# A gated decode step: work items of one head against work items of two heads, and all weights through the cache's buffers

## The chip, the cores and the metric

The kernel runs on one core of a Trainium2 chip. The metric is the device time of one execution in microseconds (us). The profile's span, from the first to the last instruction, lies a little under it.

## The reference

For two sequences (B = 2), one new token each (D = 640), the block mixes two branches with a gate. Branch `a` is attention over a cache of 4,096 positions with 32 heads of 128; branch `b` is a SiLU feed-forward layer. All data is 32-bit floats.

```python
g = sigmoid((x * gate_w).sum(-1, keepdims=True))
# a: x [2,1,640], k_cache and v_cache [2,32,4096,128], wq [640,4096], wo [4096,640]
q = (x @ wq).reshape(B, 1, H, Dh).transpose(0, 2, 1, 3)
scores = einsum("bhqd,bhkd->bhqk", q, k_cache) * Dh ** -0.5
o = einsum("bhqk,bhkd->bhqd", softmax(scores), v_cache)
a = o.transpose(0, 2, 1, 3).reshape(B, 1, H * Dh) @ wo
# b: w1 [640,1728], w2 [1728,640]
b = silu(x @ w1) @ w2
out = g * a + (1 - g) * b
```

The two caches are 268.4 MB of the 298 MB that are read.

## The kernel before, in words

A work item is one head of one sequence, so there are 64 items, ordered by head and then by sequence. An item's K is 4,096 x 128 numbers, laid out as 128 partitions with 32 consecutive positions each, so every partition takes one contiguous run of 16 KB; V is laid out the same way. `load_k` (L199) and `load_v` (L207) issue these loads from SyncE's queue (SP).

For each item the kernel does this:

- `scores_mul`: the query times K, elementwise. GpSimd takes the last 8 of the 32 position columns (L220), VectorE the first 24 (L223), reading the query from PSUM.
- `scores_sum`: VectorE sums over the 128 numbers of each position (L227) and takes the maximum in each partition (L229).
- `peak` and `weights`: TensorE brings the 128 maxima into one row (L233, tile `mt`), VectorE reduces it (L235, `mx`), TensorE spreads the result to all partitions (L240, `mb`), ScalarE copies it (L242, `nb`) and computes the exponentials with their sums (L244, into the `pz` tile).
- `total` and `invert`: TensorE sums over the partitions (L256, `tot`), VectorE inverts (L261).
- `values`: 8 products of the weights with V, four position columns at a time, each to one of four groups of 32 PSUM partitions (L272, `pv`).
- `combine` and `scale`: ScalarE copies `pv` to SBUF (L283, `osb`); four small products pick the four diagonal blocks and give the head's output as a column (L286, `po`); VectorE scales it (L293).
- `project`: the output columns of both sequences times the head's 128 rows of `wo`, added to one accumulator `acc` in PSUM (L108) over all heads and over the feed-forward layer.

In the records every 32-bit matrix product is two records.

The queries of two heads are made by `queries` (L185) from `wq`, in four calls of three or two products spread over the four previous items; the columns of x are spread to 128 copies (`xb`), so that the query appears in every partition. `ffn_in` (L137) multiplies x with `w1`, in pieces of two column blocks between the items 14 and 39; `ffn_act` applies SiLU; `ffn_out` accumulates the hidden values times `w2` at the end.

There are three pools of buffers: five for K (also used for `w2` at the end), four for V, four for weights of 10 KB per partition. `wq` comes in eight loads with runs of 2 KB, `wo` in eight with runs of 2.5 KB, `w1` in four with runs of 2 KB and 768 bytes, `w2` in eight with runs of 2.5 KB. The order on every engine is written out by hand in the loop at the end of the kernel: in round i, K of item i is loaded and scored, the softmax of item i - 1 is done, and V of item i - 3 is loaded and used (`LAG = 3`). In the last round the loads of `w2` and of the last `wo` are issued, and the accumulations over them end the kernel.

Of the kernel before, what the change touches and what calls it, by code (L numbers as in the profile page):

```python
# [15 lines left out]
def tile_gated_decode(  # L16
# [12 lines left out]
    nc = tc.nc  # L29
# [16 lines left out]
    work = ctx.enter_context(tc.tile_pool(name="work", bufs=3))  # L46
# [3 lines left out]
    ps_s = ctx.enter_context(tc.tile_pool(name="ps_s", bufs=3, space=bass.MemoryType.PSUM))  # L50

# [4 lines left out]

    wq_v = wq.rearrange("(p j) n -> p j n", j=J)
    w1_v = w1.rearrange("(p j) f -> p j f", j=J)
    WQ = 4 * DH
    wq_sb = {}  # L60

    def load_wq(s):
        t = wpool.tile([P, J, WQ], F32, tag="w", name="wq_sb")
        nc.sync.dma_start(t, wq_v[:, :, s * WQ : (s + 1) * WQ])
        wq_sb[s] = t
# [5 lines left out]
    nscale = const.tile([1, P], F32, name="nscale")  # L71
    nc.vector.memset(nscale, -SCALE)
    sel = const.tile([P, 4], F32, name="sel")
    nc.vector.reduce_sum(sel, ident.rearrange("p (a b) -> p b a", b=32)[:, :4, :], axis=AX.X)
    NPZ = 4
    pz = []
# [5 lines left out]
    xb = const.tile([P, B, J, P], F32, name="xb")  # L82
    nc.vector.tensor_copy(xb, xs[:, :, :, None].to_broadcast([P, B, J, P]))
    g = const.tile([P, B], F32, name="g")
    gc = const.tile([P, B], F32, name="gc")

    def gates():
        gb = wpool.tile([P, J, P], F32, tag="w", name="gb")
# [4 lines left out]
        ge = work.tile([P, B], F32, name="ge", bufs=1)  # L93
# [8 lines left out]
    NMM = H + NF  # L102
# [14 lines left out]
    o_first = const.tile([P, 32], F32, name="o_first")  # L117
    nc.vector.memset(o_first, 0.0)

    hT = const.tile([P, NF, B], F32, name="hT")  # L120

    W1, PH = {}, {}

    def load_w1(n0, n1):
        f0, f1 = FC[n0][0], FC[n1 - 1][0] + FC[n1 - 1][1]
        t = wpool.tile([P, J, WQ], F32, tag="w", name="w1_sb")
        nc.sync.dma_start(t[:, :, : f1 - f0], w1_v[:, :, f0:f1])
        for n in range(n0, n1):
            W1[n] = t[:, :, FC[n][0] - f0 : FC[n][0] - f0 + FC[n][1]]

    def ffn_in(n0, n1):
        m = FC[n0][1]
        ph = ps_s.tile([P, 512], F32, tag="sm", name="ph")
        for n in range(n0, n1):
            c = (n - n0) * B
            for j in range(J):
                nc.tensor.matmul(  # L137
                    ph[:m, c : c + B], W1[n][:, j, :], xs[:, :, j], start=(j == 0), stop=(j == J - 1)
                )
        PH[n0] = ph  # L140

    def ffn_act(n0, n1):
        m, k = FC[n0][1], n1 - n0
        ph = PH[n0][:m, : k * B].rearrange("p (n b) -> p n b", b=B)
        e = work.tile([P, 4, B], F32, name="he", bufs=2)
        e = e[:m, :k, :]
        nc.scalar.activation(e, ph, AF.Exp, scale=-1.0)
        nc.vector.tensor_scalar_add(e, e, 1.0)
        nc.vector.reciprocal(e, e)
        nc.vector.tensor_mul(e, e, gc[:m, None, :].to_broadcast([m, k, B]))  # L150
        nc.vector.tensor_mul(hT[:m, n0:n1, :], ph, e)  # L151

    TAIL = ((NF - 1, NF), (0, 4), (4, 7), (7, 9), (9, 10), (10, 11), (11, 12), (12, 13))

    def ffn_load(n0, n1):
        if FC[n0][1] == P:
            t = kpool.tile([P, n1 - n0, D], F32, tag="k", name="w2_sb")
            nc.sync.dma_start(t, w2[n0 * P : n1 * P, :].rearrange("(n p) d -> p n d", p=P))
        else:
            f, m = FC[n0]  # L160
            t = kpool.tile([P, 1, D], F32, tag="k", name="w2_sb")
            nc.sync.dma_start(t[:m, 0, :], w2[f : f + m, :])
        return n0, n1, t

    def ffn_out(n0, n1, t):
        for n in range(n0, n1):
            m = FC[n][1]
            accumulate(hT[:m, n, :], t[:m, n - n0, :])

    items = [(h, b) for h in range(H) for b in range(B)]  # L170
    N = len(items)
    CV = C - C // 4
    LATE = H - 4
    qsb = {}
    qps, K, V, S, M, R, O, WO = {}, {}, {}, {}, {}, {}, {}, {}

    QUNITS = [(b, j0, j1) for b in range(B) for j0, j1 in ((0, 3), (3, J))]

    def queries(hp, u):
        s, lo = divmod(hp * 2 * DH, WQ)  # L180
        if u == 0:
            qps[hp] = ps_q.tile([P, B, 2 * DH], F32, name="q")
        b, j0, j1 = QUNITS[u]
        for j in range(j0, j1):
            nc.tensor.matmul(  # L185
                qps[hp][:, b, :],
                xb[:, b, j, :],
                wq_sb[s][:, j, lo : lo + 2 * DH],
                start=(j == 0),
                stop=(j == J - 1),  # L190
            )
        if u == len(QUNITS) - 1:
            qsb[hp] = work.tile([P, B, 2 * DH], F32, name="qsb", bufs=2)
            nc.scalar.copy(qsb[hp], qps[hp])  # L194

    def load_k(i):
        h, b = items[i]
        K[i] = kpool.tile([P, C, DH], F32, tag="k", name="k")
        nc.sync.dma_start(K[i], kc[b, h].rearrange("(p c) d -> p c d", c=C))  # L199

    def load_v(i):
        h, b = items[i]
        V[i] = vpool.tile([P, C, DH], F32, name="v")
        src = vc[b, h].rearrange("(p c) d -> p c d", c=C)
        step = C // 4 if i == N - 1 else C
        for c in range(0, C, step):
            nc.sync.dma_start(V[i][:, c : c + step, :], src[:, c : c + step, :])  # L207
        if h % 4 == 0 and b == 0 and h < LATE:
            load_wo(h // 4)

    def load_wo(n):
        t = wpool.tile([P, 4, D], F32, tag="w", name="wo_sb")
        nc.sync.dma_start(t, wo[4 * n * DH : 4 * (n + 1) * DH, :].rearrange("(n p) d -> p n d", p=P))
        WO[n] = t

    def scores_mul(i):
        h, b = items[i]
        lo = (h % 2) * DH
        q = qps[h // 2][:, b, lo : lo + DH]
        nc.gpsimd.tensor_mul(  # L220
            K[i][:, CV:, :], K[i][:, CV:, :], qsb[h // 2][:, b, lo : lo + DH][:, None, :].to_broadcast([P, C - CV, DH])
        )
        nc.vector.tensor_mul(K[i][:, :CV, :], K[i][:, :CV, :], q[:, None, :].to_broadcast([P, CV, DH]))  # L223

    def scores_sum(i):
        S[i] = work.tile([P, C], F32, name="s")
        nc.vector.reduce_sum(S[i], K[i], axis=AX.X)  # L227
# [3 lines left out]
    def peak(i):  # L231
        mt = ps_s.tile([P, 512], F32, tag="sm", name="mt")
        nc.tensor.matmul(mt[:1, :P], M[i], ident, start=True, stop=True)  # L233
        mx = work.tile([1, 1], F32, name="mx")
        nc.vector.reduce_max(mx, mt[:1, :P], axis=AX.X)  # L235
        M[i] = mx

    def weights(i):
        mb = ps_s.tile([P, 512], F32, tag="sm", name="mb")
        nc.tensor.matmul(mb[:, :1], nscale, M[i], start=True, stop=True)  # L240
        nb = work.tile([P, 1], F32, name="nb")
        nc.scalar.copy(nb, mb[:, :1])  # L242
        rs = work.tile([P, 1], F32, name="rs")
        nc.scalar.activation(  # L244
            pz[i % NPZ][:, :, :4],
            S[i].rearrange("p (g c) -> p g c", c=4),
            AF.Exp,
            bias=nb,
            scale=SCALE,
            accum_out=rs,  # L250
        )
        R[i] = rs

    def total(i):
        t = ps_s.tile([P, 512], F32, tag="sm", name="tot")
        nc.tensor.matmul(t[:, :1], ones, R[i], start=True, stop=True)  # L256
        R[i] = t

    def invert(i):
        r = work.tile([P, 1], F32, name="rinv", bufs=5)  # L260
        nc.vector.reciprocal(r, R[i][:, :1])  # L261
        R[i] = r

    PV = {}

    def values(i, g0, g1):
        if g0 == 0:
            PV[i] = ps_pv.tile([P, 4 * DH], F32, name="pv")
        v = V[i].rearrange("p (g c) d -> p g (c d)", c=4)
        for gr in range(g0, g1):  # L270
# [7 lines left out]
            )  # L278

    def combine(i):  # L280
        h, b = items[i]
# [117 lines left out]
```

## Time and profile before

| | us |
|---|---|
| median of 3 runs | 719.47 (719.46 to 719.49) |
| profiled execution: span | 716.6 |
| what the median has beside the span | 2.9 |
| busy: TensorE matmul / VectorE / GpSimd / ScalarE | 526.8 / 543.1 / 152.3 / 85.5 |
| mean granted TensorE clock | 0.686 |
| DMA | 298.72 MB in 33,280 packets |

The time of the profiled execution itself is given by its span; the time of the runs counts a little more at the two ends. Busy times are sums over instructions. A "group" row of the profile gives line, engine, operation, output and inputs, count, then busy us and mean ns of one, then the idle time of the engine just before these instructions and what ended most of it. A row of the timeline gives start, duration, engine, line, operation, operands and how many instructions are merged in it. The rows of stretches give for each stretch the busy time of each engine, the granted clock, the share of the 16 DMA engines' time and the rate in GB/s.

### The profile page before, as it was taken

Reading aid. Unit: us, or ns where it says so; the run is one execution under the profiler, and the core shown is the slowest. Engines: PE = TensorE matmul, PEld = TensorE weight load, DVE = VectorE, ACT = ScalarE, POOL = GpSimd, SP = SyncE. Lnnn points to the kernel's source line nnn. Section 1 sums busy time; section 2 is a strip of 40 time slices with the busy share of each in tenths; the row PEclk is TensorE's granted clock in tenths of the full one; section 3 lists DMA queues with packets and bytes.
Section 4 is the critical chain, followed back from the end, with each engine's and each line's share of the span. In section 5 each row is a group of like instructions: output and inputs, shape, how many; then the busy total and the mean of one; then the engine's idle time right before and its main releaser. Section 6 shows DMA issues by size and latency. Waiting matters only on the chain.

```text
span 716.6 us, 6927 instructions
## 1 busy us (share of the span) xinstructions
PE 526.8 (74%) x2758; PEld 283.9 (40%) x2758; DVE 543.1 (76%) x426; ACT 85.5 (12%) x282; POOL 152.3 (21%) x74
## 2 busy tenths in 40 slices
PE   2358778778767797689978776876787486785686
PEld 2234444336434273343644434432343143342233
DVE  0798989895798857978569995978787778889930
ACT  0001111101111101110011111111011011101110
POOL 0503131121312113111131221212221221222200
PEclk9655767666588765855557766688657667557668
DMA  9999999999999999999999999999999999999996
GB/s 354 412 431 426 430 418 420 421 425 433 415 423 421 427 429 414 424 420 429 431 416 423 416 431 427 420 423 429 424 428 419 423 427 431 423 429 430 424 378 251
DMA packets 33280, 298.72 MB, mean 417 GB/s; under 512 B 2968, under 2 KB 3616, under 8 KB 16992
## 3 DMA queue, kind: packets, MB, share of 16 engines
q1 hardware_dynamic: 32824, 298.27, 99.6%
q8 instruction: 22, 0.36, 0.2%
q10 hardware_dynamic: 424, 0.01, 0.0%
q14 instruction: 10, 0.08, 0.0%
HBM read 298.26 MB, written 0.01 MB: 416 GB/s over the span
## 4 chain that ended last, share of the span: by engine, by line
DMA 43%; DVE 29%; PE 24%; ACT 2%; issue 1%; SPq 1%; ACTq 0%; DVEq 0%
DMA v<-in_A_v_cache_dram 39%; DVE s L227 14%; DVE k L223 12%; PE pv L272 7%; PE q L185 6%; PE ph L137 4%; PE po L286 3%; DMA w_sb<-in_B_w_dram 3%; PE acc L108 2%; DMA wq_sb<-in_A_wq_dram 2%; PE mb L240 1%; ACT osb L283 1%; SPq L199 1%; PE mt L233 1%; ACT qsb L194 1%
## 5 line engine op out<-in xcount | busy, mean ns | idle before, releaser
L227 DVE TENSOR_REDUCE s<-k 128x32 f32<-128x4096 f32 x64 | 281.4, 4397 | 0.1
L223 DVE TENSOR_TENSOR k<-k,q 128x3072 f32<-128x3072 f32 x64 | 214.4, 3349 | 77.1 <-ACT qsb L194 53.8
L220 POOL TENSOR_TENSOR k<-k,qsb 128x1024 f32<-128x1024 f32 x64 | 150.6, 2358 | 526.8 <-DMA k<-in_A_k_cache_dram 273.2
L272 PE MATMUL pv<-v,pz 128*32 128x512 f32 x1024 | 211.9, 870 | 56.5 <-DMA v<-in_A_v_cache_dram 56.4
L185 PE MATMUL q<-wq_sb,xb 128*128 128x256 f32 x320 | 128.0, 555 | 12.6 <-DMA wq_sb<-in_A_wq_dram 12.6
L286 PE MATMUL po<-sel,osb 128*128 128x1 f32 x512 | 86.0, 289 | 21.0 <-ACT osb L283 21.0
L185 PEld LDWEIGHTS q<-wq_sb,xb 128*128 128x128 f32 x320 | 82.2, 276 | 25.6 <-issue 12.6
L286 PEld LDWEIGHTS po<-sel,osb 128*128 128x128 f32 x512 | 80.5, 240 | 27.5 <-ACT osb L283 27.2
L240 PEld LDWEIGHTS mb<-mx,nscale 1*128 1x128 f32 x128 | 27.3, 264 | 122.9 <-issue 64.7
L242 ACT COPY nb<-mb 128x1 f32<-128x1 f32 x64 | 10.2, 159 | 467.1 <-PE mb L240 467.1
L272 PEld LDWEIGHTS pv<-v,pz 128*32 128x32 f32 x1024 | 34.9, 131 | 68.6 <-issue 59.0
L235 DVE TENSOR_REDUCE mx<-mt 1x1 f32<-1x128 f32 x64 | 17.5, 274 | 52.6 <-PE mt L233 52.6
L240 PE MATMUL mb<-mx,nscale 1*128 1x1 f32 x128 | 32.7, 322 | 33.4 <-DVE mx L235 33.2
L256 PEld LDWEIGHTS tot<-rs,ones 128*128 128x128 f32 x128 | 23.6, 231 | 77.9 <-issue 41.4
L233 PE MATMUL mt<-ident,m 128*1 128x128 f32 x128 | 33.2, 354 | 18.1 <-DVE rinv L261 16.8
L283 ACT COPY osb<-pv 128x512 f32<-128x512 f32 x64 | 37.5, 586 | 59.2 <-PE pv L272 59.2
L108 PE MATMUL acc<-wo_sb,oT 128*2 128x160 f32 x248 | 19.5, 406 | 28.1 <-DVE oT L293 27.9
L256 PE MATMUL tot<-rs,ones 128*128 128x1 f32 x128 | 29.1, 296 | 1.4 <-ACT pz L244 1.4
L137 PE MATMUL ph<-xs,w_sb 128*128 128x2 f32 (+1 forms) x140 | 26.6, 321 | 4.6 <-DVE hT L151 4.6
L137 PEld LDWEIGHTS ph<-xs,w_sb 128*128 128x128 f32 (+1 forms) x140 | 26.2, 289 | 4.8 <-issue 4.8
L233 PEld LDWEIGHTS mt<-ident,m 128*1 128x1 f32 x128 | 9.7, 97 | 40.1 <-DVE rinv L261 19.7
L293 DVE TENSOR_SCALAR oT<-po,rinv,g 128x1 f32<-128x1 f32 x62 | 16.1, 260 | 12.4 <-PE po L286 12.4
(37 smaller groups left out, 99.6 us busy)
## 6 DMA issues: line engine op xcount, KB each, us to landing
k<-in_A_k_cache_dram SPq DMA_DIRECT2D x64, 2048.0 KB, 36.1
v<-in_A_v_cache_dram SPq DMA_DIRECT2D x63, 2048.0 KB, 34.5
wq_sb<-in_A_wq_dram SPq DMA_DIRECT2D x8, 1280.0 KB, 37.6
wo_sb<-in_A_wo_dram SPq DMA_DIRECT2D x8, 1280.0 KB, 29.2
w_sb<-in_B_w_dram SPq DMA_DIRECT2D x4, 1280.0 KB, 11.8
v<-in_A_v_cache_dram SPq DMA_DIRECT2D x4, 512.0 KB, 18.2
w_sb<-in_B_w_dram SPq DMA_DIRECT2D x4, 320.0 KB, 9.5
w_sb<-in_B_w_dram SPq DMA_DIRECT2D x1, 960.0 KB, 15.9
```

The costliest lines, as they stand in the source:

```text
L108: nc.tensor.matmul(acc[32 * n : 32 * n + m, :], lhsT, w[:, n * W : (n + 1) * W], start=(done[0] == 0), stop=(done[0] == NMM - 1),)
L137: nc.tensor.matmul(ph[:m, c : c + B], W1[n][:, j, :], xs[:, :, j], start=(j == 0), stop=(j == J - 1))
L185: nc.tensor.matmul(qps[hp][:, b, :], xb[:, b, j, :], wq_sb[s][:, j, lo : lo + 2 * DH], start=(j == 0), stop=(j == J - 1),)
L220: nc.gpsimd.tensor_mul(K[i][:, CV:, :], K[i][:, CV:, :], qsb[h // 2][:, b, lo : lo + DH][:, None, :].to_broadcast([P, C - CV, DH]))
L223: nc.vector.tensor_mul(K[i][:, :CV, :], K[i][:, :CV, :], q[:, None, :].to_broadcast([P, CV, DH]))
L227: nc.vector.reduce_sum(S[i], K[i], axis=AX.X)
L233: nc.tensor.matmul(mt[:1, :P], M[i], ident, start=True, stop=True)
L240: nc.tensor.matmul(mb[:, :1], nscale, M[i], start=True, stop=True)
L256: nc.tensor.matmul(t[:, :1], ones, R[i], start=True, stop=True)
L272: nc.tensor.matmul(PV[i][32 * q : 32 * q + 32, :], pz[i % NPZ][:, gr, :], v[:, gr, :], start=(gr < 4), stop=(gr >= NG - 4),)
L283: nc.scalar.copy(osb.rearrange("p c d -> p (c d)"), PV[i])
L286: nc.tensor.matmul(po[:, :1], osb[:, c, :], sel[:, c : c + 1], start=(c == 0), stop=(c == 3))
```

## The change

A work item is now two neighbouring heads of one sequence: 32 items. The 2 x 4,096 positions lie in 128 partitions with 64 consecutive positions each, head one in partitions 0 to 63 and head two in 64 to 127, and each partition takes one contiguous run of 32 KB.

All large loads go through one pool of five slabs of 34,560 bytes per partition, in a fixed order (`stream`); `pump` issues the next load as soon as the program has passed the last use of the load five places earlier (`spend`). The order is: wq for six pairs of heads, w1, then K and V of each item in turn, with wq's second chunk after item 7, three groups of wo after item 13, wq's third chunk after item 18, and after the last item three groups of wo, w2 and two groups of wo. V of an item follows its K at once. The last 64 rows of w2 come in a load of their own at the end. Weights are laid out so that a partition's run is contiguous: wq 4 or 6 KB, wo 10 KB, w1 34,560 bytes (all of a partition's five rows), w2 33,280 bytes (13 rows).

The computation follows. VectorE multiplies columns 0 to 23, then (after the step on the maximum of the item before) 24 to 43; GpSimd takes 20 columns. The maximum is taken for each half of the partitions; `mb` is made by two products, and the exponentials by two activations of 64 partitions. `values` has 16 products per item, with the two heads' weights in different columns. `po` has two columns.

The queries are made as rows (`query_rows`, 32 columns of weights, up to 512 columns of wq at a time), for a whole chunk of wq at once, and one small product per sequence and pair of heads spreads them over the partitions (`query`). `ffn_in` does all of w1 at once before the first item, reading the weight columns `n:FM:FR` at a step of 13, since w2 is now laid out with 13 rows per partition. For wo with four rows per partition, `project` works on a group of four heads and reorders the heads' outputs with 16 small products against columns `n:P:4` of the identity (`pp`), a copy by ScalarE (`oP`), and then accumulates. `project(0..2)` is called in round 14, all others after the loop. The core of the diff:

```diff
-    kpool = ctx.enter_context(tc.tile_pool(name="kpool", bufs=5))
-    vpool = ctx.enter_context(tc.tile_pool(name="vpool", bufs=4))
-    wpool = ctx.enter_context(tc.tile_pool(name="wpool", bufs=4))
+    slabs = ctx.enter_context(tc.tile_pool(name="slabs", bufs=SLOTS))
...
+    stream = [("wq", 0), ("w1", 0)]
+    for i in range(N):
+        stream += [("k", i), ("v", i)]
+        if i == 7:
+            stream.append(("wq", 1))
+        if i == 13:
+            stream.append(("wo", 0))
+        if i == 18:
+            stream.append(("wq", 2))
+    stream += [("wo", 1), ("w2", 0), ("wo", 2)]
...
+    def pump():
+        while nxt[0] < len(stream):
+            m = nxt[0]
+            if m >= SLOTS and stream[m - SLOTS] not in spent:
+                return
+            t = slabs.tile([P, SLAB], F32, tag="slab", name=stream[m][0])
+            sub(*stream[m], t)
...
+    def ffn_in():
+        w = T["w1", 0].rearrange("p (j f) -> p j f", j=J)
...
+                cols = w[:, j, n:FM:FR] if n < FR else w[:, j, FM:F]
...
+        spend("w1", 0)
...
+    def query_rows(n, part):
...
+                    nc.tensor.matmul(
+                        ps[32 * hh : 32 * hh + 32, : (e - s) * DH],
+                        xz[:, j, :],
+                        w[:, j, s:e, hh, :],
...
+    def project(grp):
+        pp = ps_s.tile([P, 512], F32, tag="sm", name="pp")
+        for n in range(4):
+            for h in range(4):
+                nc.tensor.matmul(
+                    pp[32 * h : 32 * h + 32, n * B : (n + 1) * B],
+                    ident[:, n : P : 4],
+                    O[grp][:, h, :],
...
+        nc.scalar.copy(oP[:, :, :B], pp[:, : 4 * B].rearrange("p (n b) -> p n b", b=B))
...
+    gates()
+    query_rows(0, 0)
+    query_rows(0, 1)
+    query(0)
+    ffn_in()
+    late = {
+        8: [lambda: query_rows(1, 0), lambda: query_rows(1, 1)],
+        14: [lambda: project(0), lambda: project(1), lambda: project(2)],
+        19: [lambda: query_rows(2, 0), lambda: query_rows(2, 1)],
+    }
+    for i in range(N + 1):
+        if i < N:
+            mul(i, 0)
+        if i >= 1:
             peak(i - 1)
+            weights(i - 1)
+        if i < N:
+            mul(i, 1)
+            scores(i)
+            if i + 1 < N and items[i + 1][1] == 0:
+                query(items[i + 1][0])
+        if i >= 1:
             total(i - 1)
+            values(i - 1)
+            combine(i - 1)
+            invert(i - 1)
+            scale(i - 1)
         for f in late.get(i, []):
             f()
+    for grp in range(3, 6):
+        project(grp)
+    nc.sync.dma_start(w2t, w2[FM:, :])
+    ffn_out()
+    project(6)
+    project(7)
+    accumulate(hT[:FT, FR, :], w2t)
```

More of the change, by code (lines that the diff above doesn't have):

```diff
@@ L50, in tile_gated_decode, with sub, spend @@
     ps_s = ctx.enter_context(tc.tile_pool(name="ps_s", bufs=3, space=bass.MemoryType.PSUM))
+    order = ctx.enter_context(tc.manual_schedule())
+    items = [(hp, b) for hp in range(HP) for b in range(B)]
+    N = len(items)
+    QCH = ((0, 6), (6, 12), (12, HP))
+    WOG = ((0, 3), (3, 6), (6, 8))
+    stream = [("wq", 0), ("w1", 0)]
[8 more added lines that the diff above has]
+    stream += [("wo", 1), ("w2", 0), ("wo", 2)]
+    T = {}
+    spent = set()
+    nxt = [0]
+    def sub(what, n, t):
+        if what in ("k", "v"):
+            hp, b = items[n]
+            src = (kc if what == "k" else vc)[b, 2 * hp : 2 * hp + 2]
+            nc.sync.dma_start(
+                t[:, : C * DH], src.rearrange("h s d -> (h s d)").rearrange("(p c) -> p c", p=P)
+            )
+        elif what == "wq":
+            p0, p1 = QCH[n]
+            w = (p1 - p0) * 2 * DH
+            nc.sync.dma_start(
+                t[:, : J * w].rearrange("p (j n) -> p j n", j=J),
+                wq.rearrange("(p j) n -> p j n", j=J)[:, :, p0 * 2 * DH : p1 * 2 * DH],
+            )
+        elif what == "w1":
+            nc.sync.dma_start(t[:, : J * F], w1.rearrange("(p j) f -> p (j f)", j=J))
+        elif what == "w2":
+            nc.sync.dma_start(t[:, : FR * D], w2[:FM, :].rearrange("(p n) d -> p (n d)", n=FR))
+        else:
+            g0, g1 = WOG[n]
+            for g in range(g0, g1):
+                nc.sync.dma_start(
+                    t[:, (g - g0) * 4 * D : (g - g0 + 1) * 4 * D],
+                    wo[g * 4 * DH : (g + 1) * 4 * DH, :].rearrange("(p n) d -> p (n d)", n=4),
+                )
+    def pump():
[5 more added lines that the diff above has]
+            sub(*stream[m], t)
+            T[stream[m]] = t
+            nxt[0] += 1
+    def spend(what, n):
+        spent.add((what, n))
+        pump()
     xs = const.tile([P, B, J], F32, name="xs")
@@ L70, in tile_gated_decode @@
     nc.vector.memset(ones, 1.0)
[L71 to L76, printed above, removed]
+    nsc = const.tile([1, 2, P], F32, name="nsc")
+    nc.vector.memset(nsc, 0.0)
+    for hh in range(2):
+        nc.vector.memset(nsc[:, hh, hh * HALF : (hh + 1) * HALF], -SCALE)
+    sel = const.tile([P, 8], F32, name="sel")
+    nc.vector.reduce_sum(sel, ident.rearrange("p (a b) -> p b a", b=32)[:, :8, :], axis=AX.X)
+    spread = const.tile([HALF, B, P], F32, name="spread")
+    for b in range(B):
+        for hh in range(2):
+            nc.vector.tensor_copy(
+                spread[:, b, hh * HALF : (hh + 1) * HALF],
+                ident[:HALF, 32 * hh + b : 32 * hh + b + 1].to_broadcast([HALF, HALF]),
+            )
+    NPZ = 2
+    pz, rs2 = [], []
     for i in range(NPZ):
@@ L115, in accumulate @@
         done[0] += 1
[L117 to L129, printed above, removed]
@@ L153, in tile_gated_decode @@
[L153 to L163, printed above, removed]
@@ L196, in load_k @@
[L196 to L209, printed above, removed]
@@ new lines, in ffn_in, with ffn_out @@
+        spend("w1", 0)
+    def ffn_out():
+        w = T["w2", 0]
+        for n in range(FR):
+            accumulate(hT[:, n, :], w[:, n * D : (n + 1) * D])
+        spend("w2", 0)
+    qrow, qps, qsb = {}, {}, {}
+    def query_rows(n, part):
+        p0, p1 = QCH[n]
+        np_ = p1 - p0
+        w = T["wq", n][:, : J * np_ * 2 * DH].rearrange("p (j q h d) -> p j q h d", j=J, h=2, d=DH)
+        if part == 0:
+            qrow[n] = work.tile([HALF, 6 * DH], F32, name="qrow")
+        s, e = ((0, 4), (4, np_))[part]
+        if e > s:
+            ps = ps_s.tile([P, 512], F32, tag="sm", name="qr")
+            for j in range(J):
+                for hh in range(2):
+                    nc.tensor.matmul(
+                        ps[32 * hh : 32 * hh + 32, : (e - s) * DH],
+                        xz[:, j, :],
+                        w[:, j, s:e, hh, :],
+                        start=(j == 0),
+                        stop=(j == J - 1),
+                    )
+            nc.scalar.copy(qrow[n][:, s * DH : e * DH], ps[:HALF, : (e - s) * DH])
+        if part == 1:
+            spend("wq", n)
@@ new lines, in query @@
+    def query(hp):
+        n = next(k for k, (a, z) in enumerate(QCH) if a <= hp < z)
+        c = (hp - QCH[n][0]) * DH
+        qps[hp] = ps_q.tile([P, B, DH], F32, name="q")
+        for b in range(B):
+            nc.tensor.matmul(
+                qps[hp][:, b, :], spread[:, b, :], qrow[n][:, c : c + DH], start=True, stop=True
+            )
+        qsb[hp] = work.tile([P, B, DH], F32, name="qsb")
+        nc.scalar.copy(qsb[hp], qps[hp])
+    CA, CV = 24, 44
+    S, M, R, PV, PO, O = {}, {}, {}, {}, {}, {}
@@ new lines, in kview, with mul @@
+    def kview(i):
+        return T["k", i][:, : C * DH].rearrange("p (c d) -> p c d", d=DH)
+    def mul(i, part):
+        hp, b = items[i]
+        k = kview(i)
+        if part == 0:
+            nc.gpsimd.tensor_mul(
+                k[:, CV:, :], k[:, CV:, :], qsb[hp][:, b, None, :].to_broadcast([P, C - CV, DH])
+            )
+        c0, c1 = ((0, CA), (CA, CV))[part]
+        nc.vector.tensor_mul(
+            k[:, c0:c1, :], k[:, c0:c1, :], qps[hp][:, b, None, :].to_broadcast([P, c1 - c0, DH])
+        )
@@ L296, in scale @@
-        if b == B - 1 and h < LATE:
-            project(h)
-    def project(h):
-        accumulate(O[h, 0], WO[h // 4][:, h % 4, :])
-    early, late, after = {}, {}, {}
-    for k, w in enumerate(((0, 4), (4, 8), (8, 12), (12, NF))):
-        early[8 * k + 12] = [lambda w=w: load_w1(*w)]
-    for k, p in enumerate(((0, 2), (2, 4), (4, 6), (6, 8), (8, 10), (10, 12), (12, 13), (13, NF))):
-        t = 8 * (k // 2) + 14 + k % 2
-        late.setdefault(t, []).append(lambda p=p: ffn_in(*p))
-        after.setdefault(t + 1, []).append(lambda p=p: ffn_act(*p))
@@ new lines, in scale @@
+        hp, b = items[i]
+        grp = hp // 2
+        if grp not in O:
+            O[grp] = const.tile([P, 4, B], F32, name=f"oT{grp}")
+        h = 2 * (hp % 2)
+        nc.vector.scalar_tensor_tensor(
+            O[grp][:, h : h + 2, b], PO[i][:, :2], g[:, b : b + 1], R[i], op0=ALU.mult, op1=ALU.mult
+        )
+    def project(grp):
[6 more added lines that the diff above has]
+                    O[grp][:, h, :],
+                    start=True,
+                    stop=True,
+                )
+        first = done[0] == 0
+        oP = o_first if first else work.tile([P, 4, B], F32, name="oP")
+        nc.scalar.copy(oP[:, :, :B], pp[:, : 4 * B].rearrange("p (n b) -> p n b", b=B))
+        n0 = next(k for k, (a, z) in enumerate(WOG) if a <= grp < z)
+        w = T["wo", n0][:, (grp - WOG[n0][0]) * 4 * D : (grp - WOG[n0][0] + 1) * 4 * D]
+        for n in range(4):
+            accumulate(oP[:, n, :] if done[0] == 0 else oP[:, n, :B], w[:, n * D : (n + 1) * D])
+        if grp == WOG[n0][1] - 1:
+            spend("wo", n0)
@@ L362, in tile_gated_decode @@
         for f in late.get(i, []):
             f()
-    for h in range(LATE, H - 1):
-        project(h)
-    scale(N - 1)
-    ffn_out(*tail[2])
-    project(H - 1)
-    for part in tail[3:]:
-        ffn_out(*part)
+    for grp in range(3, 6):
[5 more added lines that the diff above has]
+    accumulate(hT[:FT, FR, :], w2t)
     ot = const.tile([P, W], F32, name="ot")
```

214 lines of the change are left out of this document (63 added, 151 removed).

## The prediction, made before the changed kernel was run

> **What bounds the kernel now.** I read the page first: busy shares, transfer rate, packets, chain.
>
> ```profile
> span 716.6 us, 6927 instructions
> PE 526.8 (74%) x2758; PEld 283.9 (40%) x2758; DVE 543.1 (76%) x426; ACT 85.5 (12%) x282; POOL 152.3 (21%) x74
> GB/s 354 412 431 426 430 418 420 421 425 433 415 423 421 427 429 414 424 420 429 431 416 423 416 431 427 420 423 429 424 428 419 423 427 431 423 429 430 424 378 251
> DMA packets 33280, 298.72 MB, mean 417 GB/s; under 512 B 2968, under 2 KB 3616, under 8 KB 16992
> q1 hardware_dynamic: 32824, 298.27, 99.6%
> DMA 43%; DVE 29%; PE 24%; ACT 2%; issue 1%; SPq 1%; ACTq 0%; DVEq 0%
> ```
>
> The loads of the SP queue fill 99.6% of the sixteen DMA engines' time; VectorE and TensorE reach 76% and 74%. So the kernel lasts as long as its 298.27 MB take, plus a start and an end. The shares of the chain (VectorE 29%, TensorE 24%) are links between transfers already queued; they set no time while the engines are full. The rate is not flat, so I asked for three stretches: nearly all of it, a stretch in which only the caches load, and the end.
>
> ```profile
> core 0: us, PE busy (x) PEld busy (x) DVE busy (x) ACT busy (x) POOL busy (x), PEclk, DMA share, GB/s
> 0.70:678.00 677.30, 498.69 (x2503) 271.13 (x2503) 533.54 (x413) 82.04 (x272) 150.43 (x70) 0.68 1.01 423
> 566.00:678.00 112.00, 80.12 (x403) 37.95 (x402) 92.34 (x67) 14.52 (x47) 26.63 (x12) 0.66 1.01 428
> 678.00:712.70 34.70, 27.67 (x249) 12.69 (x248) 9.25 (x13) 3.49 (x10) 1.68 (x1) 0.70 0.94 358
> ```
>
> Cache runs of 16 KB go at 428 GB/s. With the weights among them it is 423: 677.3 x (1 - 423/428) = 7.9 us. At the end the rate is 358 and the engines' share 0.94: 34.7 x (1 - 358/428) = 5.7 us, from short runs and from loads that wait for a buffer. After the last landing only the last accumulation, the copy and the store are left:
>
> ```profile
> 692.00 18.11 SPq L158 DMA_DIRECT2D w_sb<-in_B_w_dram  x6
> 712.79 0.46 PE L108 MATMUL acc<-w_sb,hT 128*2 128x160 f32 x8 [0.34 <-DMA w_sb<-in_B_w_dram]
> 713.66 0.66 SPq L375 DMA_DIRECT2D out_dram<-ot  x1
> ```
>
> The first row shows the queue held for 18.11 us over six issues of w2. From the last accumulation (713.25) to the end of the span are 3.4 us. The median of the runs, 719.47, is 2.9 us above the span, and I keep that difference.
>
> **Part 1, the transfers.** The pieces of the weights loaded before 678 us: wq 8 x 640, w1 2,560, wo 7 x 512, together 11,264. The 7.9 us are 7.9 x 16 / 11,264 = 11.2 ns of an engine for each. I take this as the fixed price of a run. The cache's 16,384 runs become 8,192 of 32 KB: 8,192 x 11.2 / 16 = 5.7 us saved, if a run stays one piece (ends: 0, and 7 with all rounding one way). The weights become 1,920 runs for wq, 1,024 for wo, 128 for w1, 192 for w2: 3,264, where the same bytes in 16 KB runs would be 1,821, so 1,443 x 11.2 / 16 = 1.0 us. All bytes at 428 GB/s are 696.9 us; 696.9 - 5.7 + 1.0 = 692.2, or 431 GB/s. Begun at 0.7 us, the last landing comes at 693 instead of 712.7, if the queue never waits (698 if longer cache runs bring nothing).
>
> The Trainium skill ("DMA: Bandwidth & Descriptors", section "Why small descriptors are slow (HBM only)") gives a fixed cost of about 3 cycles a packet; at that page's 850 MHz this is an estimate of 3.5 ns, and the cache's saving would be 1.8 us instead of 5.7. The 11.2 ns worked out from the trace speak against it.
>
> **Part 2, the engines inside the stream.** An item now has two heads: 8.39 MB, 19.5 us of transfer.
>
> ```profile
> L227 DVE TENSOR_REDUCE s<-k 128x32 f32<-128x4096 f32 x64 | 281.4, 4397 | 0.1
> L223 DVE TENSOR_TENSOR k<-k,q 128x3072 f32<-128x3072 f32 x64 | 214.4, 3349 | 77.1 <-ACT qsb L194 53.8 <-DMA k<-in_A_k_cache_dram 22.9
> L220 POOL TENSOR_TENSOR k<-k,qsb 128x1024 f32<-128x1024 f32 x64 | 150.6, 2358 | 526.8 <-DMA k<-in_A_k_cache_dram 273.2 <-ACT qsb L194 229.5 <-DVE m L229 13.5
> L283 ACT COPY osb<-pv 128x512 f32<-128x512 f32 x64 | 37.5, 586 | 59.2 <-PE pv L272 59.2
> ```
>
> VectorE: 3.35 for the first 24 columns, 2.8 for the next 20 (5/6 of 3,349 ns), 8.8 for the sum over 64: with the small steps 15.7 us, under 19.5. GpSimd: 20 columns are 2.5 x 2.36 = 5.9, beside VectorE's 6.5. The 128 us of TensorE's query products go, and other small products come; all of that is hidden while the queue is full. What can break the cover is the ring: five slabs for everything, and each issue on SP waits until the load five places earlier is spent, with all later loads behind it. A load must be spent within four loads (39 us) of landing, less some 2 us of issue (estimate; the store above takes 2.9 from issue to the end). Rows of TensorE at its fast and slow clock:
>
> ```profile
> 603.89 1.06 PE L272 MATMUL pv<-v,pz 128*32 128x512 f32 x8 [0.69 <-DMA v<-in_A_v_cache_dram]
> 682.22 1.94 PE L272 MATMUL pv<-v,pz 128*32 128x512 f32 x8 [3.40 <-DMA v<-in_A_v_cache_dram]
> 698.03 1.05 PE L286 MATMUL po<-sel,osb 128*128 128x1 f32 x8 [0.70 <-ACT osb L283]
> 687.24 1.87 PE L286 MATMUL po<-sel,osb 128*128 128x1 f32 x8 [0.19 <-ACT osb L283]
> 705.50 1.00 PE L108 MATMUL acc<-wo_sb,oT 128*2 128x160 f32 x24 [0.20 <-DMA wo_sb<-in_A_wo_dram]
> 707.95 1.78 PE L108 MATMUL acc<-w_sb,hT 128*2 128x160 f32 x24 [1.45 <-DMA w_sb<-in_B_w_dram]
> 251.58 2.75 PE L137 MATMUL ph<-xs,w_sb 128*128 128x2 f32 x20
> 176.02 4.40 PE L137 MATMUL ph<-xs,w_sb 128*128 128x2 f32 x20 [1.13 <-DVE hT L151]
> ```
>
> A record of values is 0.13 to 0.24 us, of po 0.13 to 0.23, of acc 0.042 to 0.074, of ph 0.14 to 0.22. An item's cache slabs are spent in time: K after 16 us; V after 9.7 (the next K), 3.6 of mul, some 3 to the weights, 32 value records (4.2 to 7.8, say 6): 22 us. Two places are tight. *Start:* wq and w1 land by 21.4; all of `ffn_in`, 140 records at 0.14 to 0.22 (say 0.19) is 27 us, to 48; its activation stands on VectorE ahead of the first item's mul, to 51, although K0 landed at 31. Item 0 ends at 66.5, values(0) near 79.5, the issue of k3 is good at 81.7, and the queue runs dry at 79.8: 2 us lost (0 to 8). *Item 14:* three `project` calls hold the wo slab: the next K 9.7 + 16.5 + three times 4.2 (below) + 2 = 40.8 us against 38.9: 2 us lost (0 to 4). Together 4 us (0 to 10); last landing 697.
>
> **Part 3, the end.** After K31 there still come v31, wo (3.93 MB), w2 (4.26), wo (2.62), the rest of w2: 15.2 MB, 35 us. K31 lands at 662. What follows on the engines is one chain, since `project(3..5)`, `ffn_out`, `project(6..7)` stand behind item 31 on TensorE's queue:
>
> ```profile
> 602.82 0.38 PE L233 MATMUL mt<-ident,m 128*1 128x128 f32 x2
> ...
> 689.66 0.28 DVE L235 TENSOR_REDUCE mx<-mt 1x1 f32<-1x128 f32 x1 [0.24 <-PE mt L233]
> 691.26 0.58 PE L240 MATMUL mb<-mx,nscale 1*128 1x1 f32 x2
> 691.88 0.16 ACT L242 COPY nb<-mb 128x1 f32<-128x1 f32 x1 [4.69 <-PE mb L240]
> 692.07 0.32 ACT L244 ACTIVATE pz<-s,nb 128x32 f32<-128x32 f32 x1
> 692.30 0.19 ACT L244 ACTIVATION_READ_ACCUMULATOR pz<-s,nb 128x1 f32 x1
> 693.64 0.41 PE L256 MATMUL tot<-rs,ones 128*128 128x1 f32 x2
> ```
>
> Scores 15.7; mt 0.4, mx 0.3, mb twice 0.6, nb 0.2, two exps of 0.5, tot 0.4: 19.2. Values 6, osb 0.6, po 1.5: 27.3. Then accumulations: five groups x 32, 104, 8 = 272 records x 0.058 (between the two acc rows) = 15.8. The transposes `pp`, new: 5 x 32 = 160 records with 32 columns of weights and 2 moving. The trace has no such product; below it stands acc (0.042), above it ph (0.22, with four times the weight columns); I take acc's middle, 0.058, since four column groups are used as there: 9.3. ScalarE's copy, which TensorE waits for five times, 0.5 each: 2.5. End 3.4. Sum 58 us: the span ends at 662 + 58 = 720, some 23 us after the last landing, where before it was 4. With TensorE at the fast rows the sum is 49, at the slow ones 67.
>
> Forecast: 720 + 2.9 = **723 us**. The stream wins 16 to 20 us and the end gives 19 back.
>
> **Rivals.** *TensorE stays fast (faster).* The queue never waits and the end takes 49 to 53: 693 - 35 + 51 + 2.9 = 712, up to 717 with some slow stretches; I take 714. It decides at 58.6 us for waits and end together (716.6 - 658), only 3 below my 62. For it: acc runs fast at 705.50; against it: the clock of 0.66 to 0.70 in all three stretches, and the slow ph rows, which follow small products.
> *The first layer's weights load slowly.* `ffn_in` now reads its weight columns at a step of 13 elements, where the old ones lie side by side. At double time its records take 0.27 to 0.44, in all about 49 us, to 71. Then k2, due at 60, starts at 73, v2 some 8 us late, k3 2 more: 23 us lost where I count 4, so 723 + 19 = 742. No row shows a strided weight load, so it can't be excluded.
> The Trainium skill ("SBUF — State Buffer", section "Door 1: The DMA port swizzle (why `[64,N]` ≈ `[32,N]`)") speaks for this: accesses that each cross into a new 16-byte line pay a penalty, and the step of 13 elements is 52 bytes. No run here shows it so far.
> *Long runs gain nothing.* The cache goes at 428 or a little under, as when a run is cut in two: last landing 702, everything later by 5 to 9: 728 to 732, I take 730. The 11.2 ns rest on weights alone, which is against my own sum.
>
> **How the numbers follow.** Forecast 0.46 (its own range 716 to 732); fast TensorE 0.26; slow first layer 0.14; no gain of long runs 0.14. About 0.2% (1.4 us) is what a measurement can tell: 718.0 to 720.9 is "same". Faster comes from the fast rival nearly whole and the forecast's lower edge: 0.29. Same: 0.11. Slower: 0.60. The range 710 to 742 takes in the first, second and fourth cases but for their corners.
>
> **What would show it.** Right: packets near 13,000; a rate of 431 in the middle; the last landing near 697; waits of values or k for DMA near 80 us and around item 15 only; then 20 us and more with no DMA, TensorE at acc and pp. Wrong: a ph record over 0.25 us with k2 late; a stretch of caches at 428 or less; acc and pp at 0.04 us a record in the end.

## The result and the profile after

The changed kernel takes 720.93 us (720.13 to 721.66, 14 runs); the kernel before 719.15 (718.44 to 720.49, 14 runs). The ratio is 1.0022, with a 95% interval of 1.0015 to 1.0030: slower, by about 1.6 us, where 723 against 719.47, 3.5 us, was forecast. The sign was right, and two parts of the sum, K31's landing and the end, were off by 12 and 14 us in opposite directions. The page of the changed kernel first:

```profile
span 718.5 us, 5865 instructions
PE 372.0 (52%) x2474; PEld 189.5 (26%) x2474; DVE 501.2 (70%) x247; ACT 63.4 (9%) x225; POOL 181.8 (25%) x44
GB/s 354 432 438 409 236 409 437 427 431 426 416 442 437 427 431 429 434 417 441 431 430 431 431 421 432 430 434 424 433 434 431 432 425 433 434 431 429 422 429 153
DMA packets 13162, 298.64 MB, mean 416 GB/s; under 512 B 1672, under 2 KB 1680, under 8 KB 3664
q1 hardware_dynamic: 12712, 298.26, 97.1%
```

The packets fell from 33,280 to 13,162, and the transfer engines' busy share fell from 99.6% to 97.1%. The rate is higher nearly everywhere, but the fifth slice (236) and the last (153) have holes. The stretches of the changed kernel show them closer (columns as before):

```profile
0.70:10.00 9.30, 1.77 (x9) 1.77 (x9) 2.92 (x11) 1.28 (x1) 1.81 (x8) 1.00 0.85 295
70.00:94.00 24.00, 11.27 (x54) 4.90 (x54) 23.71 (x10) 1.99 (x7) 5.63 (x1) 0.57 0.66 259
70.00:74.00 4.00, 0.00 (x0) 0.00 (x0) 4.00 (x1) 0.00 (x0) 0.00 (x0) 0.50 0.33 139
74.00:78.00 4.00, 0.59 (x2) 0.11 (x2) 3.97 (x3) 0.00 (x0) 0.00 (x0) 0.50 0.45 123
86.00:90.00 4.00, 3.48 (x20) 0.59 (x12) 4.00 (x1) 0.44 (x1) 2.64 (x1) 0.66 0.33 135
94.00:674.00 580.00, 284.60 (x1700) 127.43 (x1700) 447.04 (x203) 54.23 (x194) 157.31 (x28) 0.65 1.00 430
340.00:380.00 40.00, 25.09 (x295) 12.57 (x294) 32.18 (x15) 4.71 (x19) 12.39 (x3) 0.67 1.00 430
700.00:712.00 12.00, 10.20 (x345) 8.00 (x349) 0.22 (x1) 0.66 (x4) 0.00 (x0) 1.00 0.59 238
708.00:712.00 4.00, 3.69 (x122) 2.99 (x121) 0.00 (x0) 0.17 (x1) 0.00 (x0) 1.00 0.11 40
```

From 70 to 94 us 6.2 MB moved where 10.3 would have at 430 GB/s: 9.6 us of transfer are lost in two holes, seen best in the rows from 70 to 78 and from 86 to 90. After that the stream runs at 430 up to 674, also at item 14 (340 to 380). The timeline shows who held the queue:

```profile
23.95 34.62 PE L202 MATMUL ph<-xs,w 128*128 128x2 f32 x140 [1.29 <-DMA w<-in_B_w_dram]
34.95 5.61 POOL L271 TENSOR_TENSOR k<-k,qsb 128x2560 f32<-128x2560 f32 x1 [32.33 <-DMA k<-in_A_k_cache_dram]
58.82 1.11 DVE L210 TENSOR_SCALAR he<-he 128x26 f32<-128x26 f32 x1 [47.49 <-ACT he L209]
61.68 6.07 DVE L275 TENSOR_TENSOR k<-k,q 128x3072 f32<-128x3072 f32 x2
67.85 8.69 DVE L281 TENSOR_REDUCE s<-k 128x64 f32<-128x8192 f32 x1
76.56 0.33 SPq L80 DMA_DIRECT2D v<-in_A_v_cache_dram  x1
83.06 6.42 PE L325 MATMUL pv<-v,pz 128*32 128x512 f32 x32
89.55 0.33 SPq L80 DMA_DIRECT2D k<-in_A_k_cache_dram  x1
```

GpSimd starts on K0 at 34.95, so K0 was there. VectorE starts on it at 61.68, because the SiLU steps of the first layer stand ahead of it in its queue. Before the first of them VectorE stood idle for 47.49 us, until TensorE's 140 records were done. K0's slab is spent at 76.56 and V0's at 89.55, and only then go the loads v2 and k3, which were due near 70 and 80. The end, from K31's landing on:

```profile
674.11 3.35 DVE L275 TENSOR_TENSOR k<-k,q 128x3072 f32<-128x3072 f32 x1 [3.32 <-DMA k<-in_A_k_cache_dram]
692.63 0.58 PE L312 MATMUL tot<-rs,ones 128*128 128x2 f32 x2 [1.17 <-ACT pz L301]
693.15 5.17 PE L325 MATMUL pv<-v,pz 128*32 128x512 f32 x32
700.02 0.66 PE L356 MATMUL pp<-oT,ident 128*32 128x2 f32 x32
700.75 0.17 ACT L365 COPY oP<-pp 128x8 f32<-128x8 f32 x1 [1.76 <-PE pp L356]
700.97 1.27 PE L184 MATMUL acc<-wo,oP 128*2 128x160 f32 x32 [0.28 <-ACT oP L365]
714.75 0.45 PE L184 MATMUL acc<-w2t,hT 64*2 64x160 f32 x8
```

From 674.1 to the end of the span are 44.4 us. A group of 32 accumulations takes 1.27 us (0.040 a record), its 32 transposes 0.66 (0.021), at a granted clock of 1.00 (row of 700 to 712). After 708 only 0.16 MB still moved, so the end of the span lies some 10 us behind the transfers.

### The profile page after: what moved, and what is told of

Read it like the earlier page. It is cut to its first block, busy times and chain, and to the rows that moved or that the text cites. A ratio compares the mean times of both kernels' runs of the same rounds, so it can differ in the third digit from the quotient of the medians.

```text
span 718.5 us, 5865 instructions
## 1 busy us (share of the span) xinstructions
PE 372.0 (52%) x2474; PEld 189.5 (26%) x2474; DVE 501.2 (70%) x247; ACT 63.4 (9%) x225; POOL 181.8 (25%) x44
## 2 busy tenths in 40 slices
DMA packets 13162, 298.64 MB, mean 416 GB/s; under 512 B 1672, under 2 KB 1680, under 8 KB 3664
## 3 DMA queue, kind: packets, MB, share of 16 engines
q1 hardware_dynamic: 12712, 298.26, 97.1%
## 4 chain that ended last, share of the span: by engine, by line
DMA 53%; DVE 25%; PE 19%; ACT 1%; issue 1%; SPq 0%; DVEq 0%; ACTq 0%
DMA k<-in_A_k_cache_dram 50%; DVE k L275 12%; DVE s L281 12%; PE pv L325 8%; PE ph L202 5%; DMA w<-in_B_w_dram 3%; PE acc L184 2%; PE mb L296 1%; PE q L253 1%; PE tot L312 1%; ACT pz L301 1%; PE pp L356 1%; DVE mx L290 1%; PE po L339 0%; DVE he L210 0%
## 5 line engine op out<-in xcount | busy, mean ns | idle before, releaser
L271 POOL TENSOR_TENSOR k<-k,qsb 128x2560 f32<-128x2560 f32 x32 | 179.8, 5618 | 497.4 <-DMA k<-in_A_k_cache_dram 419.5
L281 DVE TENSOR_REDUCE s<-k 128x64 f32<-128x8192 f32 x32 | 278.0, 8686 | 3.7
L325 PE MATMUL pv<-v,pz 128*32 128x512 f32 x1024 | 183.5, 881 | 0.0
L296 PE MATMUL mb<-mx,nsc 1*128 1x1 f32 x128 | 31.4, 345 | 217.8 <-DVE mx L290 217.8
L296 PEld LDWEIGHTS mb<-mx,nsc 1*128 1x128 f32 x128 | 28.7, 309 | 230.1 <-DVE mx L290 224.8
L339 PE MATMUL po<-sel,osb 128*128 128x2 f32 x256 | 33.7, 254 | 22.9 <-ACT osb L336 22.9
L339 PEld LDWEIGHTS po<-sel,osb 128*128 128x128 f32 x256 | 31.0, 191 | 53.4 <-ACT osb L336 53.4
L202 PE MATMUL ph<-xs,w 128*128 128x2 f32 (+1 forms) x140 | 34.6, 385 | 1.3 <-DMA w<-in_B_w_dram 1.3
L202 PEld LDWEIGHTS ph<-xs,w 128*128 128x128 f32 (+1 forms) x140 | 34.5, 347 | 1.5 <-DMA w<-in_B_w_dram 1.5
L301 ACT ACTIVATE pz<-s,nb 64x64 f32<-64x64 f32 x64 | 22.1, 345 | 1.4
```

What stands on the lines that cost most here:

```text
L202: nc.tensor.matmul(ph[:m, n * B : (n + 1) * B], cols, xs[:, :, j], start=(j == 0), stop=(j == J - 1))
L271: nc.gpsimd.tensor_mul(k[:, CV:, :], k[:, CV:, :], qsb[hp][:, b, None, :].to_broadcast([P, C - CV, DH]))
L281: nc.vector.reduce_sum(S[i], kview(i), axis=AX.X)
L296: nc.tensor.matmul(mb[:, :1], nsc[:, hh, :], M[i][:, hh : hh + 1], start=(hh == 0), stop=(hh == 1))
L301: nc.scalar.activation(pz[i % NPZ][lo:hi, :, 4 * hh : 4 * hh + 4], S[i][lo:hi].rearrange("p (g c) -> p g c", c=4), AF.Exp, bias=nb[lo:hi], ...
L325: nc.tensor.matmul(PV[i][32 * q : 32 * q + 32, :], pz[i % NPZ][:, gr, :], v[:, gr, :], start=(gr < 4), stop=(gr >= NG - 4),)
```

## The experiments

The theory after this reading had three parts: the holes come from VectorE's order (A1), a cache run has a fixed price of some 10 ns (A2), and the end is TensorE's chain behind K31 (A3). Ratios are to the kernel before, run beside each, with 95% intervals; the changed kernel's is 1.0022.

**SiLU steps later.**

```diff
     def ffn_in():
...
+        spend("w1", 0)
+        PH.append(ph)
...
+    def ffn_act():
...
     late = {
+        0: [ffn_act],
```

> The SiLU steps of the first layer on VectorE and ScalarE move from ahead of item 0's products to behind item 0's sums; nothing else changes. Theory A: the two holes in the transfers of the changed kernel between 70 and 94 us (about 9.6 us of transfer lost) come from VectorE's queue, where item 0 stands behind these steps until 61.7 us although its K landed at 35; so K0's and V0's slabs come free late. Then both holes go, K31 lands 9 to 10 us earlier, the end stays as it is: 711.5 us (709.5 to 713.5). Rival: TensorE itself, busy with the first layer until 58.6 us and holding w1's slab, is what delays the loads; then a hole of most of that size stays (later by at most the 3 us of the SiLU steps): 718 to 721 us.

Measured: 710.98 us (5 runs), ratio 0.9890 (0.9872 to 0.9909). Timeline and stretch of this run:

```profile
24.05 34.62 PE L202 MATMUL ph<-xs,w 128*128 128x2 f32 x140 [1.13 <-DMA w<-in_B_w_dram]
35.33 6.09 DVE L281 TENSOR_TENSOR k<-k,q 128x3072 f32<-128x3072 f32 x2 [23.99 <-DMA k<-in_A_k_cache_dram]
59.12 0.38 SPq L80 DMA_DIRECT2D v<-in_A_v_cache_dram  x1
73.96 0.33 SPq L80 DMA_DIRECT2D k<-in_A_k_cache_dram  x1
664.18 3.35 DVE L281 TENSOR_TENSOR k<-k,q 128x3072 f32<-128x3072 f32 x1 [3.69 <-DMA k<-in_A_k_cache_dram]
```

```profile
70.00:94.00 24.00, 14.64 (x86) 5.64 (x78) 23.50 (x12) 2.21 (x7) 5.95 (x2) 0.71 1.01 435
```

Item 0 is worked on as soon as K0 is there, while TensorE takes 34.62 us as before; v2 and k3 go at 59 and 74, and both holes are gone. K31 is there 9.9 us earlier (664.18 against 674.11). A1 holds, and TensorE's length alone is ruled out as the cause.

**Weight columns side by side.**

```diff
-                cols = w[:, j, n:FM:FR] if n < FR else w[:, j, FM:F]
+                cols = w[:, j, n * P : (n + 1) * P] if n < FR else w[:, j, FM:F]
```

> The first layer reads its weight columns side by side instead of at a step of 13 elements; the hidden units then meet other rows of w2, so the feed-forward part of the output is another one. Theory A (the step makes the weight loads dearer): a record falls from 247 ns to the 220 ns of the kernel before at the half clock, the 140 records from 34.6 to 30.8 us, everything up to k3 comes 3.8 us sooner, and the lost transfer time falls from 9.6 to 5.8: 717.1 us (716 to 718.5). Rival (the step costs nothing, the half clock alone explains the 247 ns): no change, 720.9 us (720 to 722).

Measured: 713.36 us (5 runs), ratio 0.9904 (0.9887 to 0.9922): a gain of 7.6 where 3.8 was expected. Timeline and stretch of this run:

```profile
24.01 28.10 PE L202 MATMUL ph<-xs,w 128*128 128x2 f32 x140 [0.70 <-DMA w<-in_B_w_dram]
54.30 6.07 DVE L275 TENSOR_TENSOR k<-k,q 128x3072 f32<-128x3072 f32 x2
```

```profile
70.00:94.00 24.00, 14.12 (x75) 6.86 (x78) 23.64 (x11) 3.03 (x12) 6.08 (x2) 0.64 0.96 401
```

The 140 records take 28.1 us instead of 34.6: 0.201 each, less than the slow rows of the kernel before, so I had taken the step's price too low. VectorE reaches item 0 7.4 us earlier, about the gain, and between 70 and 94 us only 24 x (1 - 401/430) = 1.6 us of transfer are lost instead of 9.6. With the step of 13 elements the whole layer takes 23% longer. That is an average over two clocks: the last section shows that the strided records took about 0.25 us at either clock, the others 0.11 at the full and 0.21 at half the clock.

**Both at once.** The two edits above together.

> The SiLU steps moved as in act_later, and the first layer's weight columns read side by side as in unit_step (so its hidden units meet other rows of w2). Theory A: the step of 13 costs time only through VectorE's queue and w1's slab; with the SiLU steps moved the queue of loads runs dry nowhere after 10 us, so a shorter first layer gains nothing: 711.0 us (710 to 712). Rival (the step itself delays the loads through w1's slab, which is spent at 58.7 us where k2 is due near 60): a further gain of 2 to 7 us, 704 to 709.

Measured: 712.70 us (5 runs), ratio 0.9916 (0.9902 to 0.9929), the same as `act_later` or a little above, and 0.7 us over the expected range. So the step of 13 costs nothing by itself; it was paid for only through VectorE's queue. The loss needs both, the long layer and VectorE's order: either change alone takes all or most of it away.

**Shorter cache runs.**

```diff
-            nc.sync.dma_start(
-                t[:, : C * DH], src.rearrange("h s d -> (h s d)").rearrange("(p c) -> p c", p=P)
-            )
+            flat = src.rearrange("h s d -> (h s d)").rearrange("(p c) -> p c", p=P)
+            step = C * DH // 2
+            for c in range(0, C * DH, step):
+                nc.sync.dma_start(t[:, c : c + step], flat[:, c : c + step])
```

> Every K and V load is issued as two loads of half of each partition's run, so that the cache moves in runs of 16 KB again; all else as in the changed kernel. Theory A (a run costs 11.2 ns of an engine, as the prediction took it): 8,192 more runs are 5.7 us of the sixteen engines; the loads before the hole at 70 us are covered by it, so some 4.7 us show: 725.6 us (724.5 to 727). By the 3.5 ns worked out from the Trainium skill's page on DMA it would be 722.4. Rival (the long runs gain nothing, the faster stream is all due to the weights): 720.9 us (720 to 722).

Measured: 725.19 us (5 runs), ratio 1.0079 (1.0066 to 1.0091). The next one cuts in four, with the SiLU steps moved:

> With the SiLU steps moved, so that no hole covers anything, every K and V load is issued as four loads of a quarter of each partition's run: runs of 8 KB, 24,576 more. Theory A (a fixed price for a run): at the 9.6 ns that the rates of the 16 KB and 32 KB runs give (427 against 430 GB/s) 14.7 us more than 711.0: 725.5 us; at the prediction's 11.2 ns 728: 724 to 728. Rival (no fixed price; only the sizes under a few KB are dear, or the number of loads in the queue matters): 711 to 717 us, or over 730.

Measured: 725.84 us (4 runs), ratio 1.0079 (1.0053 to 1.0106). The same stretch of `act_later`, `runs16` and `act_runs8`, runs of 32, 16 and 8 KB:

```profile
110.00:660.00 550.00, 265.50 (x1598) 118.47 (x1598) 417.46 (x187) 50.59 (x181) 151.68 (x27) 0.65 1.00 431
```

```profile
110.00:660.00 550.00, 269.16 (x1614) 121.21 (x1618) 422.65 (x192) 52.02 (x187) 147.75 (x27) 0.66 1.01 427
```

```profile
110.00:660.00 550.00, 264.01 (x1557) 116.53 (x1558) 408.03 (x185) 50.01 (x180) 147.25 (x27) 0.64 1.01 421
```

431, 427 and 421 GB/s. By the medians 24,576 more runs cost 14.9 us: 14.9 x 16 / 24,576 = 9.7 ns each; by the ratios (1.0079 against 0.9890), which allow for the different chips, it is 13.6 us or 8.9 ns. The 8,192 of `runs16` cost 4.3 us with the start's holes in the way. Not all of this time is transfer. Item 31 in `act_later` first, then item 31 and the end in `act_runs8`:

```profile
682.68 0.58 PE L318 MATMUL tot<-rs,ones 128*128 128x2 f32 x2 [1.17 <-ACT pz L307]
```

```profile
696.42 0.58 PE L319 MATMUL tot<-rs,ones 128*128 128x2 f32 x2 [1.17 <-ACT pz L308]
705.52 2.31 PE L185 MATMUL acc<-wo,oP 128*2 128x160 f32 x32 [0.29 <-ACT oP L372]
```

```profile
705.50:708.00 2.50, 2.48 (x60) 1.57 (x64) 0.00 (x0) 0.00 (x0) 0.00 (x0) 0.50 0.92 388
```

Item 31 comes 13.7 us later, behind 24,192 of the added runs (all but those of V31): 9.1 ns each. The rest of the longer span is the end, whose first group of accumulations took 2.31 us at a clock of 0.50 instead of 1.27 at 1.00. A2 holds with 9 to 10 ns for the prediction's 11.2, and the rival that long runs gain nothing is out.

**No transposes in the end.** `project` accumulates the heads' outputs directly for all groups but the first; the output is then another one.

> The small transposes and ScalarE's copy ahead of every accumulation group but the first are left out; the accumulations take the heads' outputs directly, so they pair outputs with other rows of wo. Theory A: the end is one chain on TensorE from K31's landing (674 us) to 715.2, and each of the five groups in it takes 1.97 us of which 1.27 are the accumulations: 5 x 0.70 = 3.5 us less, 717.4 us (716.5 to 718.5). Rival: the last landing sets the end, TensorE only fills the time up to it: no change, 720.9 us (720 to 722).

Measured: 715.89 us (5 runs), ratio 0.9947 (0.9935 to 0.9960): 5.0 us less, and 0.6 below the expected range. Its span is 714.1 with K31 at 673.53, 0.6 us earlier, so the end lasts 40.6 us instead of 44.4: 3.8 for an expected 3.5. A3 holds, but only just, for TensorE now waits 1.15 us for the last landing:

```profile
699.24 3.44 PE L184 MATMUL acc<-wo,oT 128*2 128x160 f32 x96
709.04 1.27 PE L184 MATMUL acc<-wo,oT 128*2 128x160 f32 x32 [1.15 <-DMA wo<-in_A_wo_dram]
```

**A version with both gains.** The SiLU steps moved, and the five groups of wo at the end loaded with one row per partition, so that no transposes are needed.

```diff
+                ) if g < 3 else nc.sync.dma_start(
+                    t[:, (g - g0) * 4 * D : (g - g0 + 1) * 4 * D].rearrange("p (n d) -> p n d", d=D),
+                    wo[g * 4 * DH : (g + 1) * 4 * DH, :].rearrange("(n p) d -> p n d", p=P),
+                )
...
+        if grp >= 3:
...
+            for h in range(4):
+                accumulate(O[grp][:, h, :], w[:, h * D : (h + 1) * D])
...
```

> The SiLU steps stand behind item 0's sums, as in the run before, and the five groups of wo at the end are loaded with one row per partition (runs of 2.5 KB), so that the accumulations take the heads' outputs without transposes and copies. Theory A: with the queue never empty, the end is TensorE's chain from K31's landing (664.2 us with the SiLU steps moved); without the transposes it is shorter by the 5.0 us that leaving them out took off, and the 1,920 more runs lie behind K31: 711.0 - 5.0 = 706.0, and if the last landing now sets the end (35.3 us of transfer behind K31, 1.2 for the shorter runs, 4 from the last landing to the end: 664 + 40.5 + 2.5) 707: 705.5 to 708 us. Rival: the end is set by the last landing already, and shorter runs make it later: 711 to 713 us.

Measured: 709.00 us (4 runs), ratio 0.9846 (0.9831 to 0.9861): 1.8% less than the changed kernel (by the ratios) and 1.5% less than the one before, but 1 us over the expected range. Timeline and last stretch:

```profile
657.67 13.35 SPq L100 DMA_DIRECT2D wo<-in_A_wo_dram  x1
694.70 3.71 PE L187 MATMUL acc<-w,hT 128*2 128x160 f32 x104
701.83 1.75 PE L187 MATMUL acc<-wo,oT 128*2 128x160 f32 x32 [1.11 <-DMA wo<-in_A_wo_dram]
```

```profile
702.00:707.00 5.00, 2.23 (x40) 0.83 (x32) 0.32 (x1) 0.00 (x0) 0.00 (x0) 0.55 0.00 1
```

TensorE waits 1.11 us for the last group of wo; from its landing to the end of the span (707.4) are 5.6 us, where I had allowed 4. The clock had fallen to 0.55 there, and the last group took 1.75 us instead of 1.27. One issue of shorter runs also holds SP for 13.35 us. The last run takes 768 of those runs back:

> As the run called both, but only the three groups of wo that come first at the end have one row per partition (runs of 2.5 KB, no transposes); the last two groups have runs of 10 KB and the transposes again. In the run called both TensorE waited 1.11 us for the last group of wo, which landed at 701.8 us; theory A says the end is now set by that landing: 768 runs fewer behind K31 bring it 0.5 us earlier, and the two groups' transposes take 1.4 us on TensorE, mostly ahead of it: 708.3 to 709.5 us. Rival (TensorE's chain still sets the end): 1.4 us later, 710.4 us.

Measured: 708.89 us (4 runs), ratio 0.9860 (0.9844 to 0.9877), inside theory A's range and no better than `both`:

```profile
701.91 2.31 PE L187 MATMUL acc<-wo,oP 128*2 128x160 f32 x32 [0.89 <-DMA wo<-in_A_wo_dram]
```

Its TensorE waits 0.89 us for the last group, so the landing sets this end too, and the group then takes 2.31 us, as at half the clock in `act_runs8`. What the 768 runs alone are worth is not shown by this run.

## Why the prediction was right or wrong, step by step

- *Transfers (part 1): the rate was right, the price of a run a little high.* 13,162 packets for "near 13,000", 430 GB/s for 431. A run cost 9 to 10 ns, not 11.2. The 7.9 us that were laid on the weights' pieces hold the slow start of the kernel before:

```profile
0.70:10.00 9.30, 0.00 (x0) 0.00 (x0) 0.73 (x4) 1.28 (x1) 1.50 (x6) 1.00 0.87 312
```

That is 9.3 x (1 - 312/428) = 2.5 us which the pieces did not cause; the other 5.4 make 7.7 ns by the same sum. The 3.5 ns estimated from the Trainium skill ("DMA: Bandwidth & Descriptors", "Why small descriptors are slow (HBM only)") are too low here by this measurement.
- *Start of part 2: the order was right, the price of the strided weights was not.* The step that failed is "140 records at 0.14 to 0.22 (say 0.19) is 27 us", which puts the step of 13 elements at nothing: it took 34.6 us, from 24 instead of 21. With it item 0 ended at 76.5 instead of 66.5, and 9.6 us of transfer were lost where 2 (0 to 8) were written. `unit_step` shows what was left out: without the step the records took 28.1 us and 1.6 us were lost, near the sum's 27 and 2. `act_later` shows that the loss came through VectorE's order. The rival of slow weight loads had the right cause and too high a price: the layer took 34.6 us, not 49. The Trainium skill's rule on 16-byte lines ("SBUF — State Buffer", "Door 1: The DMA port swizzle (why `[64,N]` ≈ `[32,N]`)") agrees in direction: about 0.25 us a record against 0.21 at half the clock and 0.11 at the full one.
- *Item 14: wrong by its 2 us.* Nothing was lost there: 430 GB/s from 340 to 380.
- *K31's landing:* 674 instead of 662. Of the 12 us, 5.6 are the larger loss (9.6 for 4), nearly 3 the first 10 us, in which the rate was 295 GB/s (the sum had begun at full rate at 0.7), 1.5 the rate of 430 for 431; about 2 I cannot place.
- *The end (part 3): the chain was right, one term was not.* To the end of `tot` 19.1 us for 19.2, values and po 6.9 for 8.1, the close 3.3 for 3.4. But accumulations, transposes and copies took 15.1 us (700.1 to 715.2) instead of 27.6: the failed step is "272 records x 0.058" and 160 more at the same price. In the end they cost 0.040 and 0.021. TensorE was at its full clock from 700 to 712, as the first rival had it, and the transposes with 32 weight columns cost half of the cheaper of the two rows I had set as their bounds. Why the clock is full here and stays at half longer in `act_runs8` is open.
- The sum: +12 at the start, -13.6 at the end. 718.5 + 2.9 = 721.4 for 723 (the profiled execution itself took 720.26, 1.8 above its span). The forecast's small slowdown was therefore the difference of two mis-sized terms, and its nearness to the measured time is no proof of the working.

Where did the expected gain go? The last landing was to come at 693 instead of 712.7 us if the queue never waited; it came near 709. Of the 16 us between, 9.6 are the two holes, 4.4 the slow first 10 us and the rate, and 2 stay unplaced. The 4 us that were left were more than lost in an end that lies some 10 us behind the transfers, where it was 4 before. Putting the holes right alone gave 10 us.

## What to carry to other kernels

When all loads share one ring in a fixed order, ask of each engine's queue what stands ahead of the first item's work: a few microseconds of unrelated steps on VectorE, waiting for TensorE, held two slabs and so all later loads. Each run has a small fixed price (9 to 10 ns of an engine here), which can be worked out beforehand from the rates of two stretches if a slow start is left out of them; what longer runs gain shows only if the ends of the kernel stay short. Price the work behind the last landing at both clocks (the same group of accumulations took 1.27 or 2.31 us here), and check whether the chain or the landing ends last, for the gain stops where they cross.

## What the runs showed of the hardware that was not expected

TensorE was busy without a break, and its granted clock fell to half. These are the changed kernel's stretches during the first layer (weights at a step of 13), then two of `act_unit` (weights side by side):

```profile
24.00:27.00 3.00, 3.00 (x12) 3.00 (x13) 0.00 (x0) 0.00 (x0) 0.00 (x0) 1.00 1.19 513
27.00:30.00 3.00, 3.00 (x13) 3.00 (x13) 0.00 (x0) 0.00 (x0) 0.00 (x0) 0.55 0.83 360
30.00:40.00 10.00, 10.00 (x40) 10.00 (x40) 0.00 (x0) 0.00 (x0) 5.05 (x1) 0.50 1.01 434
40.00:60.00 20.00, 18.56 (x78) 18.46 (x78) 1.14 (x2) 0.19 (x1) 6.16 (x2) 0.50 1.02 437
```

```profile
24.00:27.00 3.00, 2.98 (x27) 2.98 (x27) 0.00 (x0) 0.00 (x0) 0.00 (x0) 1.00 1.01 437
30.00:40.00 10.00, 10.00 (x49) 10.00 (x48) 4.82 (x2) 0.00 (x0) 4.76 (x1) 0.50 0.98 419
```

The layer began at the full clock. With products of two moving columns the clock fell to 0.50 after some 3 us and stayed there for the remaining 30, while the accumulations and transposes at the end had 1.00 from 700 to 712. The Trainium skill ("TensorE: Matmul & The Clock Gate", "Part 1: The HAM clock gate (the "warmup" mystery)") says some 3.4 us of sustained activity release the full clock; these rows do not agree if busy time is taken for activity.

The strided records took 3/12 = 0.25 us at the full clock and 10/40 = 0.25 at half: the clock made no difference to them. Side by side it did: 3/27 = 0.11 against 10/48 = 0.21 us. So the step of 13 more than doubled a record at the full clock and added about a fifth at half. Because the clock was at half for most of the layer, the step cost 6.5 us there and not the 18 that 130 records at a difference of 0.14 us would make (an estimate from these rows).
